# Fused scan, feed-forward and expert kernel: the last block's ranks and rows queued behind the first expert tile, the second tile's split ahead of it

## The chip, the cores and the metric

The kernel runs on one core of one Trainium2 chip, as one launch. The metric is the device time of that launch in microseconds (us); for the kernel before, the median of three runs is 560.14 us (557.66 to 560.21).

## What is computed

Three stages follow one another on 3072 tokens of width 256. The first is a chunked linear recurrence per head, the second a dense feed-forward layer, the third picks one of eight experts per token and applies it:

```python
x = attn(x, a, B, C)                       # [3072, 256]
h = x @ w_in                               # [3072, 2048]
x = np.maximum(0.01 * h, h) @ w_out        # [3072, 256]
logits = x @ w_gate + modality_bias[modality_id]
e_idx = np.argmax(logits, axis=1)
gate_w = softmax(logits)[arange, e_idx]
for e in range(8):
    mask = e_idx == e
    h = np.maximum(x[mask] @ w1[e], 0.0)   # [., 1024]
    out[mask] = gate_w[mask, None] * (h @ w2[e])
```

## The kernel before, in words

**Blocks.** Tokens go through the first two stages in six blocks of 512 (`blocks`, block index `jl` = 5 for the last). `mm1(j, f)` and `mm2(j, f)` are the two feed-forward products, one hidden slice of 128 at a time. Every fp32 product is made of three products of halves: an operand is split into a high part (a copy to fp32r) and a low part (the difference), `split` at line 525: the copy is always on ScalarE, the difference on the engine that is given.

**Routing.** When a block's output is complete, `evict_y` (line 620) copies it from PSUM to `yt`, one half on ScalarE, one on VectorE. `logits` (628) makes the gate products `lp` on TensorE, copies them to `lt` on VectorE, transposes them (`l2`; `l` in the rows), and `route` (643) goes through some ten small VectorE instructions (`lg`, `mx`, `eq`, ..., `ohb`, and the gate into `ysb`) with one exponential, `ex`, on ScalarE. `ranks` (670) turns the one-hot table `ohb` into positions with eight small TensorE products `rp`, a handful of VectorE instructions and four indirect DMAs on GpSimd that put token numbers into the list `il`; it also adds the block's counts to `base`. `rows` (704) transposes the block back to token rows (`yr`), and `rows_out` (715) stores these with their gate to `yx` in DRAM, a DMA on SyncE's queue.

**Expert tiles.** The third stage works in tiles of 256 tokens of one expert. The first five (`EARLY`) are chosen from the counts of the first four blocks by `table_early`; the others are in the table `tabf` that `table_final` (768) works out on VectorE once block 5's counts are in `base`, 22 instructions on one partition. For each tile i: `m2_idx` (796) loads the tile's list on SyncE's queue and gathers its rows `xg` with two indirect DMAs on GpSimd; `m2_w` (784) loads 1 MB each of w1 and w2 into `r1` and `r2` (three buffers in all, so that a load waits for the split of an earlier one); `m2_xT` (829) transposes the rows on TensorE into the PSUM tile `xps` and splits them into `x2h` (ScalarE) and `x2l` (VectorE); `m2_split1` (814) splits w1 into `w1s`, two copies on ScalarE and two differences on VectorE; `m2_split2` (823) splits w2 into `w2s`, with one difference on VectorE and one on GpSimd; `m2_mm1` (842) is the first product, 48 matmuls in four PSUM tiles `hp`, evicted to `hh` (ScalarE) and `hl` (VectorE); `m2_mm2` (861) is the second, 48 matmuls into `o`, and the scatter of the result. Loop i runs `m2_mm1(i)`, the preparation of tile i+1, the loads of tile i+2, `m2_mm2(i)`, `m2_split2(i+1)`. In this run there are twelve tiles.

**Shared PSUM.** `lp`, `xps` and `yr` come from one pool with a single buffer (`psm`), in the order in which the program asks for them: each can be written only when the one before it has been read.

**Order.** The program is traced in the order of the code and then ordered anew for each engine by the framework's scheduler, which may put a ready instruction ahead of one that was traced earlier. An instruction that is pinned (`Q["pin"]` at line 64, through the `Pinned` proxy at 153) is queued behind the instruction that was traced just before it on its engine. The keys with `L_` hold for the code behind block 5; the letters name VectorE (v), ScalarE (s), GpSimd (g) and TensorE (t). So in this part the two ScalarE copies of `m2_split1` are pinned (`L_m2_split1`, s), as are `x2l` (`L_m2_xT`, v), all of `evict_y`, all of `table_final`, and the transposes and copies of `rows` (`L_rows`). `ranks`, `logits`, `m2_mm1`, `m2_mm2` and `m2_split2` are not.

With the numbers in `Q` ("xe" 2, "se" 8, "me" 7), lines 1000 to 1005 trace this order behind the last product of block 5: `evict_y`, `logits`, `m2_xT(1)`, `ranks`, `table_final`, `rows` twice, `m2_mm1(0)`, `rows_out`, `m2_split1(1)`. So `x2l` of tile 1 is pinned behind the last VectorE instruction of `logits`, the first `rows` transpose behind the last product of `ranks`, and the w1 copies of tile 1 behind the last `hh` of tile 0.

Of the kernel before, what the change touches and what calls it, by code (L numbers as in the profile page):

```python
# [24 lines left out]
Q = {'sg': (0, 1),  # L25
 'i00': 0,
 'i01': 1,
 'lo1': -1,
 'o00': 0,
 'o01': 4,  # L30
 'i10': 3,
 'i11': 3,
 'xe': 2,
 'se': 8,
 'me': 7,
 'sh1': -2,
 'sh': 0,
 'ld': 9,
# [40 lines left out]
         'attn_p3': 'vst',  # L79
         'attn_cd': 't',  # L80
         'L_evict_y': 'vsg',
         'L_table_final': 'vsg',
         'L_m2_split1': 's',
         'L_rows_out': 's',
         'L_m2_xT': 'v',
# [13 lines left out]
def kernel(  # L99
# [72 lines left out]
    def run(fn, args, late=""):  # L172
        for e in (v, s, g, t_):
            e.on = e.key in Q["pin"].get(late + fn.__name__, "")
        fn(*args)
        for e in (v, s, g, t_):
            e.on = False
# [429 lines left out]
    def mm2(j, f):  # L607
        n = blocks[j][1]
        if f == 0:
            y_t[j] = [psy.tile([P, 512], F32, tag="y", name="y") for _ in range(2)]  # L610
        gh, gl = g_t.pop((j, f))
        for k in range(2):
            ds = slice(k * P, (k + 1) * P)
            for i, (w, gg) in enumerate(((woh, gh), (woh, gl), (wol, gh))):
                t_.matmul(y_t[j][k], lhsT=w[:, f, ds], rhs=gg, start=(f == 0 and i == 0), stop=(f == NF - 1 and i == 2))
# [168 lines left out]
    def m2_w(i, tab, k):  # L784
        ei = nc.values_load(tab[:, 0, k:k + 1], engines=[ENG.SP], min_val=0, max_val=NE - 1, skip_runtime_bounds_check_because=WHY)
        r1 = rawp.tile([P, 2, F2], F32, tag="raw", name="r1")
        for k in range(2):
            nc.sync.dma_start(out=r1[:, k, :], in_=w1[bass.ds(ei, 1), k * P:(k + 1) * P, :].rearrange("o p f -> p (o f)"))
        r2 = rawp.tile([P, NF2, DM], F32, tag="raw", name="r2")
        for k in range(2):  # L790
            nc.sync.dma_start(
                out=r2[:, 4 * k:4 * k + 4, :], in_=w2[bass.ds(ei, 1), k * 4 * P:(k + 1) * 4 * P, :].rearrange("o (k p) f -> p (o k) f", p=P)
            )
        m2.setdefault(i, {}).update(r1=r1, r2=r2)

    def m2_idx(i, tab, k):
        vi = nc.values_load(tab[:, 1, k:k + 1], engines=[ENG.SP], min_val=0, max_val=NE * NT - T, skip_runtime_bounds_check_because=WHY)
        gi = sp.tile([P, 2], I32, tag="gi", name="gi", bufs=6)
        r = nc.sync.dma_start(out=gi, in_=il[bass.ds(vi, T), :].rearrange("(q p) o -> p (q o)", p=P))
        for w in puts:  # L800
            tc.add_manual_dep(
                r.ins, w.name, mybir.DependencyInfo(mybir.DependencyClass.Sync, mybir.DependencyReason.DATA),
                reason="the list read here",
            )
        lim = blocks[-2][0] if tab is tabe else NT + 1
        xg = late["raw2"].tile([P, 2, YW], F32, tag="xg", name="xg", bufs=6)
        for q in range(2):
            g.indirect_dma_start(
                out=xg[:, q, :], out_offset=None, in_=yx[0:lim, :],
                in_offset=IndirectOffsetOnAxis(ap=gi[:, q:q + 1], axis=0), bounds_check=lim - 1, oob_is_err=False,  # L810
            )
        m2.setdefault(i, {}).update(gi=gi, xg=xg)
# [184 lines left out]
    jl = nb - 1  # L997
    mm2(jl, NF - 2)
    mm2(jl, NF - 1)
    fin = [(evict_y, jl), (logits, jl), (ranks, jl), (table_final,), (rows, jl, 0), (rows, jl, 1), (rows_out, jl)]  # L1000
    fin.insert(Q["xe"], (m2_xT, 1))
    fin.insert(Q["se"], (m2_split1, 1))
    fin.insert(Q["me"], (m2_mm1, 0))
    for fn, *args in fin:
        run(fn, args, "L_")
    tl = [(tabe, k) for k in range(EARLY)] + [(tabf, k) for k in range(NSTAT)]
    for i in range(len(tl)):
        if i:
            run(m2_mm1, (i,), "L_")
            if i + 1 < len(tl):  # L1010
                run(m2_xT, (i + 1,), "L_")
                run(m2_split1, (i + 1,), "L_")
        if i + 2 < len(tl):
            if i + 2 >= EARLY:
                m2_idx(i + 2, *tl[i + 2])
            m2_w(i + 2, *tl[i + 2])
        run(m2_mm2, (i,), "L_" if i + 1 < len(tl) else "Z_")
        if i + 1 < len(tl):
            run(m2_split2, (i + 1,), "L_")
    u = nc.values_load(tabu, min_val=0, max_val=NFIN, skip_runtime_bounds_check_because=WHY)  # L1020

    def cond(k):
# [46 lines left out]
```

## Time and profile before

| | |
|---|---|
| median of the runs | 560.14 us (557.66 to 560.21) |
| the profiled execution's own time | 558.4 us |
| its span, first to last instruction | 556.7 us |
| TensorE busy | 524.3 us, 94% of the span |
| VectorE, ScalarE, GpSimd busy | 66%, 60%, 36% |
| mean granted TensorE clock | 0.966 of full speed |

The profile is of one execution. PE is TensorE's matmuls, PEld its weight loads, DVE is VectorE, ACT ScalarE, POOL GpSimd, SP SyncE with its DMA queue. Times count from the first instruction. A row of a timeline gives start, duration, engine, line (L163 is the proxy through which nearly all instructions go, so that tile names tell them apart), operation, output and inputs, and in brackets the idle time just before it with what ended it. The granted clock is a share of full speed: 1.00 is 2.4 GHz and 0.50 is 1.2 GHz.

### The profile page before, as it was taken

Reading aid. Unit: us, or ns where it says so; the run is one execution under the profiler, and the core shown is the slowest. Engines: PE = TensorE matmul, PEld = TensorE weight load, DVE = VectorE, ACT = ScalarE, POOL = GpSimd, SP = SyncE. Lnnn points to the kernel's source line nnn. Section 1 sums busy time; section 2 is a strip of 40 time slices with the busy share of each in tenths; the row PEclk is TensorE's granted clock in tenths of the full one; section 3 lists DMA queues with packets and bytes.
Section 4 is the critical chain, followed back from the end, with each engine's and each line's share of the span. In section 5 each row is a group of like instructions: output and inputs, shape, how many; then the busy total and the mean of one; then the engine's idle time right before and its main releaser. Section 6 shows DMA issues by size and latency. Waiting matters only on the chain.

```text
span 556.7 us, 9530 instructions
## 1 busy us (share of the span) xinstructions
PE 524.3 (94%) x3411; PEld 426.7 (77%) x3411; DVE 367.7 (66%) x698; ACT 333.4 (60%) x699; POOL 200.3 (36%) x183
## 2 busy tenths in 40 slices
PE   7979959999999999999999999999989999999991
PEld 4434636677787788878887788778879999999990
DVE  5757998867657767777576866565486566455540
ACT  5645646776667676766766675364536576566640
POOL 5536787820301021103020200640063446655431
PEclk9795998999999999999999999999989999999997
DMA  7899630322345219331540375436059766767400
GB/s 178 151 218 209 193 108 5 80 36 58 13 88 110 59 9 137 65 58 6 88 104 0 7 129 168 140 28 88 1 170 124 274 192 197 242 209 252 148 21 22
DMA packets 128311, 61.01 MB, mean 110 GB/s; under 512 B 84545, under 2 KB 120514, under 8 KB 128258
## 3 DMA queue, kind: packets, MB, share of 16 engines
q1 hardware_dynamic: 125186, 53.94, 46.1%
q0 software_dynamic: 3072, 6.41, 3.6%
q8 instruction: 29, 0.48, 0.4%
q14 instruction: 24, 0.20, 0.2%
HBM read 53.73 MB, written 6.60 MB: 108 GB/s over the span
## 4 chain that ended last, share of the span: by engine, by line
PE 77%; DVE 6%; issue 4%; ACT 4%; POOL 4%; DMA 2%; SPq 2%; another core or an unknown queue 0%; POOLq 0%; DVEq 0%; ACTq 0%
PE y L163 21%; PE h L163 21%; PE hp L163 12%; PE o L163 10%; PE psy L163 4%; PE cb L163 3%; DMA ct<-in_C_dram 1%; PE pc L163 1%; PE yr L163 1%; DVE lb L163 1%; PE pb L163 1%; ACT e L163 1%; PE xps L163 1%; SPq L358 1%; POOL gl L163 1%
## 5 line engine op out<-in xcount | busy, mean ns | idle before, releaser
L163 ACT CAST gh<-gg 128x512 fp32r<-128x512 f32 x96 | 59.6, 620 | 69.2 <-DVE gg L163 64.5
L163 PE MATMUL h<-xh,wih 128*128 128x512 f32 x192 | 79.5, 418 | 7.2 <-DVE gg L163 7.1
L163 DVE TENSOR_TENSOR gl<-gg,gh 128x512 fp32r<-128x512 f32 x80 | 57.5, 719 | 39.1 <-ACT gh L163 37.8
L163 DVE TENSOR_TENSOR gg<-sa,h 128x512 f32<-128x512 f32 x96 | 65.4, 681 | 23.4 <-ACT sa L163 21.7
L163 POOL TENSOR_SCALAR_AFFINE_SELECT e<-e 128x1024 f32<-128x1024 f32 (+1 forms) x28 | 29.3, 1048 | 138.9 <-DMA e<-cumd 90.3
L163 PE MATMUL h<-xh,wil 128*128 128x512 f32 x192 | 76.8, 400 | 1.0 <-POOL wil L163 1.0
L163 PE MATMUL y<-gl,woh 128*128 128x512 f32 x192 | 77.2, 402 | 0.4 <-POOL gl L163 0.2
L163 PE MATMUL h<-xl,wih 128*128 128x512 f32 x192 | 77.1, 401 | 0.0
L163 PE MATMUL y<-gh,wol 128*128 128x512 f32 x192 | 75.7, 394 | 0.0
L163 PE MATMUL hp<-x2h,w1s 128*128 128x256 f32 x384 | 73.3, 286 | 0.0
L163 ACT ACTIVATE sa<-h 128x512 f32<-128x512 f32 x96 | 57.2, 596 | 22.8 <-PE h L163 17.8
L163 PE MATMUL o<-w2s,hh 128*128 128x256 f32 x384 | 69.3, 285 | 0.0
L163 DVE SCALAR_TENSOR_TENSOR hl<-hp,hh 128x512 fp32r<-128x512 f32 x48 | 33.0, 691 | 52.8 <-ACT hh L163 39.4
L163 PE MATMUL y<-gh,woh 128*128 128x512 f32 x192 | 64.1, 399 | 0.0
L163 PEld LDWEIGHTS hp<-x2h,w1s 128*128 128x128 f32 x384 | 62.3, 195 | 0.6
L163 POOL TENSOR_TENSOR w2s<-r,w2s 128x1024 fp32r<-128x1024 f32 x12 | 33.5, 2789 | 73.5 <-ACT w2s L163 42.8
L163 PEld LDWEIGHTS o<-w2s,hh 128*128 128x128 f32 x384 | 58.4, 191 | 0.4 <-issue 0.4
L163 PE MATMUL hp<-x2l,w1s 128*128 128x256 f32 x192 | 54.2, 287 | 0.0
L163 ACT ACTIVATE hh<-hp 128x512 fp32r<-128x512 f32 x48 | 28.5, 597 | 42.5 <-PE hp L163 36.1
L163 ACT ACTIVATE e<-e,ncum 128x128 f32<-128x128 f32 x160 | 51.3, 395 | 3.8 <-POOL e L163 3.8
L163 PEld LDWEIGHTS h<-xh,wih 128*128 128x128 f32 x192 | 36.8, 192 | 18.8 <-DVE gg L163 10.9
L163 PE MATMUL o<-w2s,hl 128*128 128x256 f32 x192 | 51.1, 283 | 0.0
(206 smaller groups left out, 1020.2 us busy)
## 6 DMA issues: line engine op xcount, KB each, us to landing
r<-in_moe_w_dram SPq DMA_DIRECT2D x48, 512.0 KB
e<-cumd SPq DMA_DIRECT2D x20, 512.0 KB
raw<-in_moe_w_in_dram SPq DMA_DIRECT2D x4, 1024.0 KB
raw<-in_moe_w_out_dram SPq DMA_DIRECT2D x4, 1024.0 KB
yx<-ysb SPq DMA_DIRECT2D x6, 528.0 KB
xt<-in_x_dram SPq DMA_DIRECT2D x24, 128.0 KB
ct<-in_C_dram SPq DMA_DIRECT2D x24, 64.0 KB
bt<-in_B_dram SPq DMA_DIRECT2D x24, 64.0 KB
```

Of the source, the lines that this page charges most:

```text
L163: r = f(*args, **kw)
L358: nc.sync.dma_start(out=xt, in_=x[b, :, sl, :].rearrange("h p d -> p h d"))
```

## The change

The order of the code behind block 5 is written out, and some of it moves. `m2_xT(1)` is now traced ahead of `logits`; `m2_split1(1)` right behind `logits` and ahead of `m2_mm1(0)`; `ranks`, both `rows` and `rows_out` of block 5 behind `m2_mm2(0)` and `m2_split2(1)`; `table_final` behind `m2_mm2(1)` and `m2_split2(2)`, and without its pin. The other pins stay, but what stands just before a pinned instruction is new: `x2l` of tile 1 is now pinned behind `evict_y`'s VectorE copy, and the w1 copies of tile 1 behind `ex`, the exponential of block 5's routing.

```diff
- 'xe': 2,
- 'se': 8,
- 'me': 7,
...
-         'L_table_final': 'vsg',
...
-    fin = [(evict_y, jl), (logits, jl), (ranks, jl), (table_final,), (rows, jl, 0), (rows, jl, 1), (rows_out, jl)]
-    fin.insert(Q["xe"], (m2_xT, 1))
-    fin.insert(Q["se"], (m2_split1, 1))
-    fin.insert(Q["me"], (m2_mm1, 0))
-    for fn, *args in fin:
-        run(fn, args, "L_")
+    def tail(*fns):
+        for fn, *args in fns:
+            run(fn, args, "L_")
+
     tl = [(tabe, k) for k in range(EARLY)] + [(tabf, k) for k in range(NSTAT)]
+    tail((evict_y, jl), (m2_xT, 1), (logits, jl), (m2_split1, 1), (m2_mm1, 0))
     for i in range(len(tl)):
         if i:
-            run(m2_mm1, (i,), "L_")
+            tail((m2_mm1, i))
             if i + 1 < len(tl):
-                run(m2_xT, (i + 1,), "L_")
-                run(m2_split1, (i + 1,), "L_")
+                tail((m2_xT, i + 1), (m2_split1, i + 1))
         if i + 2 < len(tl):
             if i + 2 >= EARLY:
                 m2_idx(i + 2, *tl[i + 2])
             m2_w(i + 2, *tl[i + 2])
         run(m2_mm2, (i,), "L_" if i + 1 < len(tl) else "Z_")
         if i + 1 < len(tl):
-            run(m2_split2, (i + 1,), "L_")
+            tail((m2_split2, i + 1))
+        if i == 0:
+            tail((ranks, jl), (rows, jl, 0), (rows, jl, 1), (rows_out, jl))
+        if i == 1:
+            tail((table_final,))
```

## Rows read from the trace of the kernel before

**Rows 1.** Windows: busy time (instructions) of PE, PEld, DVE, ACT, POOL; PEclk, DMA, GB/s

```profile
440.00:460.00 20.00, 20.00 (x170) 20.00 (x170) 12.68 (x16) 13.31 (x19) 10.01 (x9) 1.00 0.66 212
```

**Rows 2.** Chain that ended last: start, us, what; one expert tile in steady state

```profile
431.03 0.44 PE xps L163 x4
431.47 5.75 PE o L163 x48
437.22 5.76 PE hp L163 x48
```

**Rows 3.** Timeline of PE behind block 5

```profile
405.40 0.27 PE L163 MATMUL l<-ident,lt 128*128 128x128 f32 x1
...
407.62 0.63 PE L163 MATMUL hp<-x2h,w1s 128*128 128x256 f32 x4
410.36 0.19 PE L163 MATMUL rp<-ohb,tris 128*128 128x32 bf16 x1 [2.11 <-DVE ohb L163]
...
411.24 0.65 PE L163 MATMUL yr<-ident,yt 128*128 128x128 f32 x4 [0.52 <-DVE x2l L163]
```

**Rows 4.** Windows of 2 us behind these waits (columns as in rows 1)

```profile
412.00:414.00 2.00, 2.00 (x14) 2.00 (x13) 1.20 (x8) 0.76 (x2) 1.27 (x2) 0.62 0.90 359
414.00:416.00 2.00, 2.00 (x12) 2.00 (x12) 1.23 (x4) 0.35 (x1) 1.66 (x2) 0.52 0.03 3
```

**Rows 5.** Chain that ended last, behind block 5 (columns as in rows 2)

```profile
400.18 0.34 PE lp L163 x2
...
402.15 0.64 PE lp L163 x14
...
411.89 4.60 PE hp L163 x26
```

**Rows 6.** Timeline of DVE behind block 5

```profile
399.40 0.69 DVE L163 COPY yt<-y 128x512 f32<-128x512 f32 x1 [0.41 <-PE y L163]
...
402.81 0.29 DVE L163 COPY lt<-lp 128x128 f32<-128x128 f32 x1 [1.02 <-PE lp L163]
403.02 2.35 DVE L163 TENSOR_TENSOR w1s<-r,w1s 128x1024 fp32r<-128x1024 f32 x2
405.29 3.41 DVE L163 TENSOR_TENSOR w2s<-r,w2s 128x1024 fp32r<-128x1024 f32 x1
408.62 0.18 DVE L163 TENSOR_TENSOR lg<-l,btab 128x32 f32<-128x32 f32 x1
...
410.12 0.18 DVE L163 CAST ohb<-oh 128x32 bf16<-128x32 f32 x1
...
410.52 0.66 DVE L163 TENSOR_TENSOR x2l<-xps,x2h 128x512 fp32r<-128x512 f32 x1
...
420.80 0.15 DVE L163 CAST tabf<-vb 1x14 int32<-1x14 f32 x1
```

**Rows 7.** Timeline of ACT behind block 5

```profile
400.84 1.99 ACT L163 CAST w1s<-r 128x1024 fp32r<-128x1024 f32 x2
402.72 2.00 ACT L163 CAST w2s<-r 128x1024 fp32r<-128x1024 f32 x2
...
409.50 0.23 ACT L163 ACTIVATE ex<-lg 128x32 f32<-128x32 f32 x1 [1.21 <-DVE lg L163]
```

**Rows 8.** Timeline of POOL behind block 5

```profile
404.80 2.81 POOL L163 TENSOR_TENSOR w2s<-r,w2s 128x1024 fp32r<-128x1024 f32 x1 [28.60 <-ACT w2s L163]
...
424.97 2.87 POOL L163 TENSOR_TENSOR w2s<-r,w2s 128x1024 fp32r<-128x1024 f32 x1 [7.72 <-issue]
```

**Rows 9.** Windows around a shorter wait of PE in block 5 (columns as in rows 1)

```profile
360.00:365.00 5.00, 3.72 (x23) 2.83 (x22) 2.98 (x13) 1.95 (x4) 0.12 (x1) 1.00 0.11 31
365.00:370.00 5.00, 5.00 (x24) 4.14 (x23) 3.33 (x11) 3.24 (x6) 2.61 (x3) 1.00 0.01 0
```

**Rows 10.** Timeline of SP's queue: the load of tile 2's r2, the first list read through `tabf`

```profile
405.40 0.96 SPq L791 DMA_DIRECT2D r<-in_moe_w_dram  x2
...
437.19 0.37 SPq L799 DMA_DIRECT2D gi<-il  x1
```

## The prediction

> **What bounds the kernel now.** I first read the windows over the expert stage, then one tile in the chain that ended last, then TensorE's own timeline where it falls behind that pattern, and last the other engines there. In a window of the steady stage PE is busy for all of its 20 us at full clock, while no other engine passes 14 us [rows 1]. A tile costs 5.76 us for `hp`, 5.75 us for `o` and 0.44 us for the transposes, 11.95 us in all [rows 2], and from the third tile to the last nothing but PE sets the pace. So only a loss on PE is worth removing, and there is one place behind block 5 that has one. PE has issued the first four products of tile 1 by 408.25 and then waits 2.11 us, to 410.36, for `rp`, which needs `ohb`; the `yr` transposes behind it wait 0.52 us more, to 411.24, for `x2l` to have read `xps` [rows 3]. That is **2.63 us idle**. Then the granted clock falls to 0.62 and 0.52 in the two windows behind it [rows 4], the lower of its two levels (1.2 GHz), and 26 `hp` products take 4.60 us [rows 5]. At 5.76 / 48 = 0.12 us each [rows 2] they would take 3.12 us: **1.48 us lost to the clock**. Together 4.11 us.
>
> The other engines say why. The route chain starts with `lg` at 408.62, although its transpose was done at 405.67 [rows 3, 6], because DVE stood in a w2 split that took 3.41 us: POOL had begun its own half of that split at 404.80 and held on to 407.61, and the DVE instruction ended 1.09 us after that [rows 6, 8]. `ohb` ends at 410.30, and `x2l`, pinned behind the last instruction of the route, runs from 410.52 [rows 6]. So `rp` is not alone in the way: with it gone, `hp` would still wait for `x2l` to 411.18.
>
> **The change, part by part.**
>
> *Tile 1's `x2l`* is now pinned behind `evict_y`'s DVE copy, which ends at 400.09 [rows 6]; with 0.66 us it is done near 400.8, six microseconds ahead of its use. This ends the wait for it. Its price: `lp` must now wait until `xps` has been read, so the logits start about 0.7 us later than the 400.18 of [rows 5].
>
> *`ranks` and `rows` behind tile 0's second product* (eight small products, five DVE instructions, four indirect DMAs on POOL, eight transposes, two ACT copies, one DMA on SP). PE's own work only changes place: eight `rp` and four `yr` are about 0.8 us whether they stand ahead of `hp` or in it. On POOL the puts fall into the 7.72 us that it idles before tile 2's split [rows 8]. I cost them at nothing; without that cover they would delay a split with a whole tile of slack.
>
> *`table_final`* behind the second tile and unpinned: its end moves from 420.95 [rows 6] by up to a tile, 12 us, to about 433. Queued behind its result on SP are the list load at 437.19 [rows 10] and the weight loads after it. DVE has room for it, as it is busy for 12.68 us of 20 [rows 1]. Cost nothing, with 4 us of slack; if it came later still, the loads have most of a tile before their use.
>
> *The w1 split of tile 1* is what pays. Its two ACT copies ran from 400.84, straight behind tile 0's last `hh` [rows 7], and its DVE differences were over by 405.37 [rows 6]. Now the copies are queued behind `ex`, which ended at 409.73 [rows 7], at the end of a serial chain: yt copy, `x2l`, 16 `lp`, `lt`, transpose, `lg` to the subtraction, `ex`. The trace does not have this order, so I bound it. At best each link follows at once: 400.09 + 0.66 + 0.98 (`lp`: 0.34 + 0.64) [rows 5] + 0.29 + 0.27 + 0.85 (half of the 1.68 from `lg` to the end of `ohb`) + 0.23 = 403.4 for the end of `ex` [rows 3, 6, 7]. A copy is 1.0 us and a difference 1.18 us [rows 6, 7], so all of `w1s` would be there at about 406.8, before PE wants it, and the whole 4.1 us is gained. At worst the chain takes as long as now: from 400.09 to 408.62 is 8.53 us, plus `x2l`, so `lg` at 409.3, `ex` over at 410.4 and the last difference at 413.8.
>
> I take a value between, by the nearest rows. The transpose keeps its place behind most of `o` in PE's queue: 405.40 [rows 3], plus 0.7 for `lp`, less 0.44 because the `xps` transposes now run earlier, so it ends near 405.9. `lg` then follows at 406.0, since no w1 difference is in front of it. `ex` is over at 407.1, the first w1 copy at 408.1, the second at 409.1, the first difference at 409.3, the second at 410.5. PE: from 400.18, `lp` 0.98, `o` 5.76 and the transpose 0.13 end at 407.05; `rp` wants `ohb`, 1.68 us after `lg`, so 407.7, an idle of 0.65; with `yr` it is 408.5, and `hp` has its first w1 half. From there PE may start the four PSUM tiles of `hp` in turn, as it did with four products before the wait [rows 3]: 8 products (0.96 us) need only the first copy, 12 more only the first difference and the second copy. That covers the second difference; if they go in strict order, some 1.4 us more are idle. I put the remaining **idle at 1.0 us**, so 1.6 us are gained there.
>
> *The clock.* In block 5 PE idled 1.28 us of 5, and the clock was 1.00 in that window and in the next [rows 9]; behind 2.63 us it fell [rows 3, 4]. With about 1 us I expect no fall: 1.48 us gained. The bounds are nothing and 1.48.
>
> *The weight loads.* The load of r2 for tile 2 went out at 405.40, just behind the last w1 difference [rows 6, 10], and now goes about 5 us later, with the first load of tile 3 in turn behind it on SP. Its split comes nearly a tile after that, so nothing.
>
> **Sum.** 558.4 - 1.6 - 1.5 = 555.3 us for the profiled execution. The median of the runs shown stands 1.74 us above it (560.14), so the same 3.1 us make **557.0 us**.
>
> **Rivals.**
>
> *The split is as late as `x2l` was.* If the route chain loses another microsecond or so on its way (the transpose later in PE's queue, a w2 difference in front of `lg`), the w1 differences end at about 411.5, where `x2l` now ends at 411.18. One wait takes the other's place, the idle is again 2 to 3 us and the clock falls as before: 560.1 give or take 1. For it speaks that DVE and PE are in-order and did put other work into this chain; against it, that the w1 differences are out of `lg`'s way.
>
> *The shared port.* POOL's half of the w2 split takes 2.81 us [rows 8], and DVE's half took 3.41 us beside it against 1.18 us for a w1 difference alone [rows 6]: a DVE instruction on two SBUF tiles that comes after POOL's start ends only after POOL. The w2 copies, now behind those of w1 [rows 7], are not pinned, so ACT may run them while it waits for `ex`, and POOL's half then meets a w1 difference or the DVE half ahead of `lg`. Either moves the end of `w1s` from 410.5 by up to 2.8 us; half of that, with the clock spared only in part, leaves about 1 us of gain: 559. The Trainium skill, SBUF — State Buffer, section "Who interferes with whom", says that a DVE instruction with two SBUF inputs contends with a GpSimd instruction that reads SBUF, and that whichever issues first keeps the pair for its whole length. The trace agrees with its 3.41 us.
>
> *Slower.* The place is ACT's queue between `ex` and the w1 copies. If `lg` comes at 409.3, the bound above, the first copy ends at 411.4, the first difference at 412.6 and the second at 413.8. PE idles from 408.5 to 411.4 and about 1 us more, which with 0.65 before makes 4.5 us instead of 2.63, and the low clock lasts as long again or twice as long: 1.9 to 3.4 us lost, 562 to 563.5. It decides once `lg` is later than about 408.
>
> **How the numbers follow.** Forecast 0.48 (PE out of the way by 1.5 to 4.1 us, most of it above half a per cent), late split 0.27, port 0.12, slower 0.13. Half a per cent, about what a measurement of this kernel can tell from no change, is 2.8 us. Faster 0.48, same 0.27 + 0.12 = 0.39, slower 0.13. The full 4.1 us give 556.0, and the runs before reach 2.5 us under their median, so the range starts at 554.3. Upward it takes in the late split and the port, to 561.2, and leaves out most of the slower case. The forecast alone would span 555 to 558.6.
>
> **What would show it.** Right: `x2l` of tile 1 by 401, no wait of PE for `ohb` above 1 us, the w1 copies directly behind `ex` at about 407, and a clock of 1.00 in all windows from 400 to 420. The third tile's `hp` would then begin some 3 us earlier than now. Wrong: PE waiting on `w1s` for 2 us or more, a window at 0.5 behind it, or `lg` still behind a w2 difference; SP waiting for `tabf` would show as loads and an `xg` that come late in tiles 4 and 5.

## The result and the profile after

The kernel after takes **567.53 us** (median of 4 runs, 565.98 to 568.56) beside 559.82 us for the kernel before in the same measurement (4 runs): ratio 1.0144, 95% interval 1.0108 to 1.0179. It is slower by 7.7 us, where 3.1 us of gain were predicted. The profiled execution of after took 567.43 us. Here and below a ratio takes only runs in the chip's quicker state, so it need not be that of the two medians.

The stages ahead of the change vary by nearly one per cent from profile to profile: the last `yt` copy on VectorE starts between 396.87 and 400.45 us. So I also compare the **tail**: from the start of that copy, which is block 5's, to the start of the last eviction of `o` on ScalarE. Before: 399.40 to 544.42, 145.02 us. After: 399.71 to 552.09, 152.38 us. The tail is 7.36 us longer, so the whole loss lies here.

**Behind block 5 the gain came as predicted, the split of w1 a microsecond later.** VectorE's timeline of after; the columns are start, duration, engine, line, operation, tiles, and in brackets the idle time before with what ended it:

```profile
399.71 0.69 DVE L159 COPY yt<-y 128x512 f32<-128x512 f32 x1 [0.41 <-PE y L159]
400.32 0.68 DVE L159 TENSOR_TENSOR x2l<-xps,x2h 128x512 fp32r<-128x512 f32 x1
...
407.05 0.19 DVE L159 TENSOR_TENSOR lg<-l,btab 128x32 f32<-128x32 f32 x1 [2.58 <-PE l L159]
...
409.21 1.23 DVE L159 TENSOR_TENSOR w1s<-r,w1s 128x1024 fp32r<-128x1024 f32 x1 [0.28 <-ACT w1s L159]
...
410.52 1.22 DVE L159 TENSOR_TENSOR w1s<-r,w1s 128x1024 fp32r<-128x1024 f32 x1
...
413.32 2.12 DVE L159 CAST pi<-pf 128x4 int32<-128x4 f32 x1
```

These answer to [rows 6]. `x2l` of tile 1 is over by 401.0, `lg` starts at 407.05 where it had stood behind the w2 split until 408.62, and the two w1 differences end at 410.44 and 411.74 (forecast: `lg` at 406.0, the differences over at 409.3 and 410.5). TensorE did not wait for them: its `hp` products run from 409.50 without a gap. Its timeline, which answers to [rows 3], has one wait left ahead of tile 2, and the granted clock (the third number from the end in the row of the windows, second fence) stays at 1.00 through 34 us:

```profile
408.90 0.19 PE L159 MATMUL rp<-ohb,tris 128*128 128x32 bf16 x1 [1.28 <-DVE ohb L159]
```
```profile
396.00:430.00 34.00, 31.55 (x272) 30.45 (x270) 25.53 (x58) 19.11 (x29) 15.20 (x10) 1.00 0.57 99
```

Tile 2's `hp` begins 22.65 us behind the `yt` copy (at 422.36), against 25.71 us before (at 425.11): 3.06 us gained, where 3.1 had been worked out.

**One tile later more than three times that is lost.** ScalarE's timeline of after:

```profile
424.10 0.59 ACT L159 CAST x2h<-xps 128x512 fp32r<-128x512 f32 x1
424.56 2.01 ACT L159 CAST w1s<-r 128x1024 fp32r<-128x1024 f32 x2
426.46 0.61 ACT L159 ACTIVATE hh<-hp 128x512 fp32r<-128x512 f32 x1
435.87 1.04 ACT L159 CAST w2s<-r 128x1024 fp32r<-128x1024 f32 x1 [8.80 <-DMA r<-in_moe_w_dram]
436.82 0.59 ACT L159 ACTIVATE hh<-hp 128x512 fp32r<-128x512 f32 x1
439.45 1.05 ACT L159 CAST w2s<-r 128x1024 fp32r<-128x1024 f32 x1 [2.04 <-DMA r<-in_moe_w_dram]
440.40 1.07 ACT L159 ACTIVATE hh<-hp 128x512 fp32r<-128x512 f32 x2
```

The same stretch of ScalarE's timeline before:

```profile
431.07 0.60 ACT L163 ACTIVATE hh<-hp 128x512 fp32r<-128x512 f32 x1 [0.60 <-PE hp L163]
431.56 0.58 ACT L163 CAST x2h<-xps 128x512 fp32r<-128x512 f32 x1
...
433.92 2.00 ACT L163 CAST w2s<-r 128x1024 fp32r<-128x1024 f32 x2
```

Before, all four `hh` evictions of tile 2 stand ahead of tile 3's copies `x2h`, `w1s`, `w2s`. After, these copies stand among the `hh`: `x2h` and `w1s` ahead of the first, a `w2s` copy ahead of the second and another ahead of the third. ScalarE took them in this order: the `w2s` copies wait 8.80 and 2.04 us for tile 3's w2 from DRAM, and the `hh` of tile 2 wait behind them, although their `hp` has long been there. TensorE pays; its waits (total, times, longest), and the rows of its timeline where they stand:

```profile
PE o L159 <- ACT hh L159: 7.2, 2, 6.7
PE rp L159 <- DVE ohb L159: 1.3, 1, 1.3
PE o L159 <- DVE hl L159: 1.2, 1, 1.2
```
```profile
430.00 0.39 PE L159 MATMUL o<-w2s,hl 128*128 128x256 f32 x1 [1.17 <-DVE hl L159]
...
437.46 0.80 PE L159 MATMUL o<-w2s,hh 128*128 128x256 f32 x2 [6.73 <-ACT hh L159]
...
441.04 0.80 PE L159 MATMUL o<-w2s,hh 128*128 128x256 f32 x2 [0.43 <-ACT hh L159]
```

That is 8.33 us idle. (The 1.17 us for `hl` are a wait for VectorE, where tile 3's w1 differences stand in front of it; the first took 2.54 us instead of 1.2, beside POOL's half of tile 2's w2 split from 423.55 to 427.12.)

```profile
425.66 2.54 DVE L159 TENSOR_TENSOR w1s<-r,w1s 128x1024 fp32r<-128x1024 f32 x1 [0.83 <-ACT w1s L159]
```

The clock falls behind it; windows of after (length, busy time of PE, PEld, DVE, ACT, POOL with instructions, granted clock, busy share of the DMA engines, GB/s):

```profile
422.00:424.00 2.00, 2.00 (x20) 2.00 (x19) 2.00 (x4) 2.00 (x4) 0.45 (x1) 1.00 0.76 10
424.00:426.00 2.00, 2.00 (x19) 2.00 (x18) 1.17 (x2) 2.00 (x4) 2.00 (x1) 1.00 0.93 11
...
432.00:434.00 2.00, 0.00 (x0) 0.00 (x0) 0.00 (x0) 0.00 (x0) 0.00 (x0) 0.50 1.39 130
...
436.00:438.00 2.00, 0.54 (x2) 0.54 (x3) 1.05 (x1) 1.41 (x2) 0.00 (x0) 0.50 0.51 145
438.00:440.00 2.00, 2.00 (x12) 2.00 (x11) 0.77 (x2) 0.55 (x1) 0.00 (x0) 0.50 1.01 407
440.00:442.00 2.00, 1.57 (x8) 1.27 (x8) 0.98 (x2) 1.48 (x3) 1.37 (x1) 0.54 1.05 386
```

In the last three PE is busy for 4.11 us at about half speed, so about 2 us more are lost. The account of the tail: 8.33 + 2.0 - 3.06 = 7.3 us, of 7.36 measured.

**Why the load is late** stands in the same windows: from 422 to 426 the DMA engines are 0.76 and 0.93 busy and move 10 and 11 GB/s. Four indirect DMAs, the puts of block 5's token numbers into `il`, were issued just before. POOL's timeline of after:

```profile
412.11 3.30 POOL L159 TENSOR_TENSOR w2s<-r,w2s 128x1024 fp32r<-128x1024 f32 x1 [2.72 <-ACT w2s L159]
415.72 0.99 POOL L159 DMA_INDIRECT il<-ids,pi  x1 [0.31 <-DVE nt L159]
...
419.57 0.98 POOL L159 DMA_INDIRECT il<-ids,pi  x1 [0.30 <-issue]
```

SP's queue, and the DMA issues from 402 to 446 (KB each, median us from issue to landing):

```profile
416.37 1.48 SPq L714 DMA_DIRECT2D yx<-ysb  x1
423.72 4.74 SPq L787 DMA_DIRECT2D r<-in_moe_w_dram  x2
```
```profile
r<-in_moe_w_dram SPq DMA_DIRECT2D x12, 512.0 KB, 8.8
yx<-ysb SPq DMA_DIRECT2D x1, 528.0 KB, 15.4
...
il<-ids,pi POOLq DMA_INDIRECT x4, 14.8
```

Puts and row store land 15 us behind their issue. The load of tile 3's w2 goes out at 423.72, 3.2 us behind the last put, and its halves are used at 435.87 and 439.45, the moment they land: 12 and 16 us behind 423.72. Before, the puts went out from 412.42 to 417.25 and the load at 424.47; its copies waited for nothing at 433.92. The last put on POOL and the load on SP's queue before, and the windows there:

```profile
416.27 0.98 POOL L163 DMA_INDIRECT il<-ids,pi  x1 [0.30 <-issue]
```
```profile
424.47 1.12 SPq L791 DMA_DIRECT2D r<-in_moe_w_dram  x2
```
```profile
420.00:424.00 4.00, 4.00 (x36) 4.00 (x35) 3.53 (x7) 3.48 (x5) 0.00 (x0) 1.00 0.78 26
```

So the engines were busy and moved little there too. After, the puts come 3.3 us later: POOL does its half of tile 1's w2 split first (to 415.41), and the row names `nt` on VectorE (to 415.50) as what ended the wait.

So there were two theories to test. **Order**: tracing `m2_xT(1)` ahead of the logits changes where tile 3's copies stand on ScalarE, two tiles later. **Load**: the puts make the load late. A third was that unpinned `table_final` does harm.

### The profile page after: what moved, and what is told of

Read it like the earlier page. It is cut to its first block, busy times and chain, and to the rows that moved or that the text cites. A ratio compares the mean times of both kernels' runs of the same rounds, so it can differ in the third digit from the quotient of the medians.

```text
span 565.6 us, 9524 instructions
## 1 busy us (share of the span) xinstructions
PE 529.0 (94%) x3411; PEld 426.4 (75%) x3411; DVE 366.2 (65%) x698; ACT 333.1 (59%) x699; POOL 200.8 (35%) x183
## 5 line engine op out<-in xcount | busy, mean ns | idle before, releaser
L159 PE MATMUL o<-w2s,hh 128*128 128x256 f32 x384 | 70.9, 289 | 7.2 <-ACT hh L159 7.2
L159 PEld LDWEIGHTS o<-w2s,hh 128*128 128x128 f32 x384 | 59.7, 195 | 7.7 <-ACT hh L159 7.7
L159 PEld LDWEIGHTS h<-xh,wih 128*128 128x128 f32 x192 | 36.4, 190 | 18.4 <-DVE gg L159 10.6
```

The lines of the kernel that those rows point to most:

```text
L159: r = f(*args, **kw)
```

## Experiments

Tails in us, beside the medians. A tail is read from one profiled execution; two pairs of kernels with nearly the same waits of PE (before and the ranks moved alone, after and the table pinned) have tails 0.2 and 0.4 us apart. Each ratio is to runs of the kernel before on the same chip (medians 559.41 to 560.45):

| kernel | median (runs) | ratio to before, interval | tail |
|---|---|---|---|
| before | 559.82 (4) | | 145.02 |
| after | 567.53 (4) | 1.0144, 1.0108 to 1.0179 | 152.38 |
| `x2h` pinned | 558.85 (10) | 0.9993, 0.9957 to 1.0028 | 144.28 |
| `m2_xT(1)` ahead, alone | 569.15 (4) | 1.0176, 1.0111 to 1.0242 | 154.54 |
| ranks, rows, table moved, alone | 560.17 (10) | 1.0035, 1.0000 to 1.0071 | 144.82 |
| `table_final` pinned | 567.76 (4) | 1.0150, 1.0083 to 1.0217 | 152.80 |
| no puts of block 5 | 556.40 (1) | one run | 143.17 |
| `x2h` pinned, no puts | 554.11 (1) | one run | 141.65 |
| `x2h` pinned, rows later | 557.24 (12) | 0.9957, 0.9931 to 0.9983 | 142.48 |

**The order on ScalarE put back.** In after, `m2_xT` has a pin on VectorE alone; here it pins `x2h` on ScalarE too, so the copy keeps its traced place.

```diff
-         'L_m2_xT': 'v',
+         'L_m2_xT': 'vs',
```

> The changed kernel with one pin more: ScalarE's x2h copy of each tile is queued behind the last hh of the tile before. Theory O (order: the loss comes from tile 3's x2h, w1 and w2 copies standing on ScalarE ahead of tile 2's hh, where they wait for a weight load): ScalarE goes through four hh of tile 2 first, PE's wait of 6.7 us and the low clock behind it are gone, the gain of some 3 us at tile 1 stays, so 555.5 to 557.5 us against 559.8 before. Rival L (loads: ranks, rows and the list puts moved later make the weight load itself late, whoever waits for it): the load still lands at 436 to 439, PE waits for w2s of tile 3 or for tile 2 much as now, 564 to 568. Rival T (table_final without its pin fills VectorE and holds up hl): no change, 567.

The loss is gone, and part of the gain with it: ratio 0.9993, tail 0.74 us shorter than before, where 557.5 us at most had been expected. ScalarE's timeline of this kernel shows the order restored and the load still late:

```profile
425.61 0.60 ACT L159 ACTIVATE hh<-hp 128x512 fp32r<-128x512 f32 x1 [0.24 <-PE hp L159]
426.10 0.58 ACT L159 CAST x2h<-xps 128x512 fp32r<-128x512 f32 x1
...
432.41 1.05 ACT L159 CAST w2s<-r 128x1024 fp32r<-128x1024 f32 x1 [3.83 <-DMA r<-in_moe_w_dram]
435.95 1.05 ACT L159 CAST w2s<-r 128x1024 fp32r<-128x1024 f32 x1 [2.50 <-DMA r<-in_moe_w_dram]
```

ScalarE still waits 6.33 us for tile 3's w2, but with tile 2's `hh` behind it PE loses only 1.9 us, for tile 3's `hh`. Order decides the size of the loss; the lateness of the load is a cause of its own.

**One step of the change alone.** The kernel before with one number changed, so that `m2_xT(1)` is traced ahead of `logits` and all else stays.

```diff
- 'xe': 2,
+ 'xe': 1,
```

> The kernel before with one step moved: the transposes of tile 1 traced ahead of the logits; ranks, rows and table_final stay where they were, the w1 split behind tile 0's hh. Theory O: this alone brings the order on ScalarE in which tile 3's copies stand among tile 2's hh, so PE waits in tile 2 for several us with a low clock behind it: 562 to 570. Rival L: ranks, rows and the puts are not moved, so no late load: 555 to 558, the gain at tile 1 alone. Rival T: the same 555 to 558.

This step alone loses as much as the whole change. Tile 3's copies stand among tile 2's `hh` again; ScalarE's wait for the first w2 copy and PE's for `hh` are longer than in after:

```profile
438.48 1.04 ACT L163 CAST w2s<-r 128x1024 fp32r<-128x1024 f32 x1 [10.21 <-DMA r<-in_moe_w_dram]
```
```profile
PE o L163 <- ACT hh L163: 7.8, 1, 7.8
```

PE also waits 1.8 us for `hl`, and 1.4 us for `x2l` of tile 2 in place of the wait for `ohb`. `ranks` keeps its traced place here (its first put goes out at 415.13, 2.7 us later than before), and the load is late all the same: moving `ranks` is not needed for that.

**The other moves alone.** After, with the code from `evict_y` to `m2_mm1(0)` in its old order; `ranks`, `rows` and `table_final` stay where after has them.

```diff
-    tail((evict_y, jl), (m2_xT, 1), (logits, jl), (m2_split1, 1), (m2_mm1, 0))
+    tail((evict_y, jl), (logits, jl), (m2_xT, 1), (m2_mm1, 0), (m2_split1, 1))
```

> The changed kernel with the front part put back as it was (logits, transposes of tile 1, first product of tile 0, w1 split); ranks, rows and table_final stay in their new places. Theory O: ScalarE's order has all four hh of tile 2 ahead of tile 3's copies, no wait in tile 2; x2l is again pinned behind the route, so the wait ahead of tile 1 stays: 559 to 561. Rival L: the late load comes with ranks and rows, so 564 to 568. Rival T: the unpinned table is there, 564 to 568.

No difference that can be told: tail 144.82 against 145.02. PE's waits are those of before, 2.1 us of `rp` for `ohb` and 0.5 us of `yr` for `x2l`. The `hh` of tile 2 keep their place, the puts end at 417.87 and the w2 copies of tile 3 wait for nothing.

**The table pinned again.**

```diff
+         'L_table_final': 'vsg',
```

> The changed kernel with table_final pinned again, in its new place. Theory O: ScalarE's order is that of the changed kernel, 566 to 569. Rival L: the same, 566 to 569. Rival T: the pin takes the loss away, 555 to 558.

567.76 us, as after, with a wait of `o` for `hh` of 7.7 us (after: 7.2). The third theory falls.

**The puts taken away.** After without the four puts of block 5 (its expectation says what is left out).

```diff
-        for q in range(nq):
+        for q in range(nq if j < len(blocks) - 1 else 0):
             w = g.indirect_dma_start(
```

> The changed kernel without block 5's four list DMAs (puts), so the tiles behind tile 4 work on an incomplete list; ScalarE's order is that of the changed kernel, with tile 3's w2 copies among tile 2's hh. Theory O+L (both are needed: the copies stand in front, and the weight load they wait for, issued at 423.72, lands 12 to 15 us later because the puts of 415.7 to 420.5 clog the DMA engines): the load lands some 4 us after its issue, ScalarE waits for it 1 us or less in place of 8.8, PE's wait for hh shrinks from 6.7 us to under 2, and from the last yt copy to the last o eviction it takes 143 to 146 us in place of 152.4. Rival (the order alone: the load is late since it is issued late, whatever else moves): PE's wait for hh stays above 5 us, 150 us or more.

ScalarE has the same order as after, and the loss is gone: 556.40 us in one run, tail 143.17. The first w2 copy of tile 3 waits 0.60 us instead of 8.80, the second not at all, and the windows from 422 show a load at work as soon as it is issued:

```profile
427.34 1.05 ACT L159 CAST w2s<-r 128x1024 fp32r<-128x1024 f32 x1 [0.60 <-DMA r<-in_moe_w_dram]
428.30 0.59 ACT L159 ACTIVATE hh<-hp 128x512 fp32r<-128x512 f32 x1
428.78 1.04 ACT L159 CAST w2s<-r 128x1024 fp32r<-128x1024 f32 x1
```
```profile
422.00:424.00 2.00, 2.00 (x19) 2.00 (x18) 2.00 (x4) 2.00 (x5) 0.79 (x1) 1.00 0.02 6
424.00:426.00 2.00, 2.00 (x19) 2.00 (x18) 1.14 (x2) 2.00 (x3) 2.00 (x1) 1.00 0.72 184
```

The load was issued at 423.36, within 0.4 us of after's. So its delay is the work of the puts, and the order costs little while the load is in time: PE's wait for `hh` is gone, and 1.1 us for `hl` are left.

**Both.** `x2h` pinned and no puts.

> The kernel with x2h pinned (e1), also without block 5's puts. Theory O+L: the w2 copies of tile 3 no longer wait for their load (3.83 and 2.50 us in e1), PE's wait of 1.9 us for hh of tile 3 goes; what is left is the 1.28 us wait for ohb, so 141 to 142.5 us from the last yt copy to the last o eviction, against 144.3 in e1 and 145.0 before. Rival (the load is late for another reason): 144 us as in e1, with the same waits.

554.11 us in one run, tail 141.65: 3.37 us under before, the size that the prediction gave to the change (3.1). PE waits for nothing but `ohb` (1.3 us). With this kernel the two causes can be set side by side:

| tail, us | puts | no puts |
|---|---|---|
| tile 3's copies among the `hh` | 152.38 | 143.17 |
| behind the `hh` | 144.28 | 141.65 |

Alone the order costs 1.5 us and the puts 2.6 us; together they cost 10.7. The sum of the two would be 4.1, so 6.6 us come of their meeting. The right column rests on one run of each kernel.

**The puts kept, the rows later.** `x2h` pinned, `ranks` as in after, but the rows of block 5 traced behind the preparation of tile 2, so that their store goes to SP behind the weight loads.

```diff
-         'L_m2_xT': 'v',
+         'L_m2_xT': 'vs',
...
                 tail((m2_xT, i + 1), (m2_split1, i + 1))
+            if i == 1:
+                tail((rows, jl, 0), (rows, jl, 1), (rows_out, jl))
...
-            tail((ranks, jl), (rows, jl, 0), (rows, jl, 1), (rows_out, jl))
+            tail((ranks, jl))
```

> The kernel with x2h pinned (e1), with rows and rows_out of block 5 traced behind the transposes and the w1 split of tile 2. The transposes of tile 2 no longer wait for yr, so its w1 split and with it the load of tile 3's w2 come some 3 us earlier, and the row store goes out behind the loads. Theory O+L: that load is issued before or beside the puts, lands earlier, and most of the 1.9 us wait in tile 3 goes: 142 to 143.5 us from the last yt copy to the last o eviction, 0.3 to 0.5 per cent faster than before. Rival (the puts hold up any load that is issued within some ten microseconds of them, also those ahead): 144 to 146 us, no gain.

**557.24 us**, ratio 0.9957 (0.9931 to 0.9983): the fastest of the kernels that do the whole work, 2.2 us under before in the same measurement (559.41, 17 runs) and with a tail shorter by 2.54 us. The tail fell where it was expected, and the way there only in part. Counted from the `yt` copy (400.45 here, 396.87 with `x2h` pinned alone), tile 3's w2 is issued 1.7 us earlier, where some 3 had been expected, and not ahead of the puts; its first half is used 0.4 us earlier, its second 2.6 us. SP's queue and ScalarE's timeline of this kernel:

```profile
422.85 0.97 SPq L787 DMA_DIRECT2D r<-in_moe_w_dram  x2
...
430.76 1.72 SPq L714 DMA_DIRECT2D yx<-ysb  x1
```
```profile
435.59 1.05 ACT L159 CAST w2s<-r 128x1024 fp32r<-128x1024 f32 x1 [3.47 <-DMA r<-in_moe_w_dram]
436.95 1.05 ACT L159 CAST w2s<-r 128x1024 fp32r<-128x1024 f32 x1 [0.32 <-DMA r<-in_moe_w_dram]
```

The puts end at 422.21 here, the load follows at once and still takes until 435.59. With the row store (`yx`) out of its way at 430.76 its first half is as late behind its issue as ever (12.7 us, against 11.5 with `x2h` pinned alone), so the store is not needed for that delay. ScalarE's waits sum to 3.79 us instead of 6.33, and that is enough: PE waits only 0.8 us for `ohb` and 0.2 us for an `xg`.

## Why the prediction was wrong

- **Tile 1: right in size, and in mechanism but for one link.** `x2l` by 401.0; one wait of 1.28 us for `ohb` where an idle of 1.0 in all had been put, so 1.35 us gained there instead of 1.6; the clock at 1.00, worth 1.48. These make 2.8 of the 3.06 us; the other 0.2 are not accounted for. The link is the route chain: `lg` came at 407.05, 1.05 us later than forecast, the w1 copies directly behind `ex` began at 408.14 instead of 407.1, and the second difference ended at 411.74, where the late split had put it (411.5). Yet the price that this rival put on it did not come: PE ran `hp` from 409.50 through without a wait, as the forecast had it with 8 products that need only the first copy. The gain held because PE did not need the split as early as the rival took it to. The slower rival (`lg` later than about 408) did not occur.
- **The step that failed** is the weight loads: "Its split comes nearly a tile after that, so nothing". It took the order on ScalarE behind tile 1 as given. For tile 2's load that held. But in the kernel after, tile 3's copies come up to be run at 427.1 instead of 433.9, ahead of three of tile 2's `hh`, and the slack that the sentence counted on was that order. Tracing one step ahead of the logits shifted it; the one-number experiment shows it without any other part of the change. What stood at nothing came to 8.33 us of idle PE, 7.16 of them for `hh`, and some 2 us of low clock.
- **The second step** is the puts: "On POOL the puts fall into the 7.72 us that it idles before tile 2's split", and "I cost them at nothing". They do fall into that gap (415.72 to 420.55). But the cost was sought in POOL's queue, and it lies with the DMA engines and with those who wait for a load. The same slow spell is in the trace of before (DMA engines 0.78 busy at 26 GB/s from 420 to 424), and its load landed unseen because nobody needed it until 433.9: the cover was there and was not named.
- **`table_final` at nothing: right.** Its end came at 422.56 rather than 433, and pinning it changes nothing.
- **The port.** It did act, on another instruction than the rival had named: `pi`, the last VectorE step ahead of the puts, took 2.12 us beside POOL's half of the split and ended with it, at 415.44. Since the puts stand behind that half on POOL anyway, and start at 415.72, it cost next to nothing here. It may also have cost the 1.17 us that PE waits for `hl` in tile 2: the w1 difference ahead of it, at 425.66, took 2.54 us beside POOL instead of 1.2. No run separates that from the order on VectorE.
- **The range** (to 561.2) missed because its slower rival had only one place, and no row of before was asked what else the same reordering would bring forward. Its lower end is not what its words give (556.0 less 2.5 is 553.5, not 554.3), which changes nothing here.

What stays open: why tracing `m2_xT(1)` first brings tile 3's copies forward is seen only as an order of instructions, and not explained by a run; nor is it shown by what means the puts slow the load. Leaving out the row store alone was not tried, nor a fourth weight buffer.

## What to carry to other kernels

When a step moves in traced order, look a tile or two further on at each in-order engine: a copy that needs a load, placed in front of evictions that TensorE needs, can turn a late load into idle time. Here ScalarE's waits of 10.84 us left TensorE 7.2 us without `hh`, while behind the evictions waits of 6.33 us cost it 1.9. Cost a small scatter by what the DMA engines do for the next 15 us, not by the queue that issues it. And two delays that are each cheap alone should be priced together if one stands in front of the other's cover.

## What the hardware showed that was not expected

**Behind four scatters of 128 numbers a load took three times as long.** With the puts, 11.5 to 13.5 us pass in five kernels from the issue of tile 3's w2 to the use of its first half; without them, in the same order on ScalarE, 4.0 us. DMA queues of after from 420 to 428 (packets, MB, time of the packets as a share of 16 engines):

```profile
q1 hardware_dynamic: 439, 0.46, 107.1%
```

and of the kernel without puts in the same stretch:

```profile
q1 hardware_dynamic: 1339, 1.39, 55.9%
```

Times 16 engines and 8 us, that is 137 us for 439 packets and 72 us for 1339: **0.31 and 0.053 us a packet**, on a queue that isn't that of the puts, with packets of about 1 KB in both. With the rows later, where the row store goes out only at 430.76, the same stretch of the queue reads

```profile
q1 hardware_dynamic: 393, 0.48, 40.4%
```

which is 0.13 us a packet: part of the 0.31 may go with the row store, and the load is late without it. With puts, the first half of tile 3's w2 comes 13.4 to 18.4 us behind the end of the last put in five kernels, whether it was issued 0.6 or 4.9 us behind it. The Trainium skill, DMA: Bandwidth & Descriptors, section "Specifications", gives 512 B as the least transfer for line rate and says that the engine reads, modifies and writes below it. The puts are of 4 bytes each, and the runs agree that they are dear, but don't tell that cause from another.

**The clock** stayed at 1.00 behind 1.28 us of idling and behind 1.17 more, 21 us later, until the idle time of 6.73 us; it then stood at 0.50 into the window from 440, more than 2.5 us after PE was at work again.
